# Splitting two of the seven products of a second layer once more, with their sums on GpSimd

## The chip, the cores and the metric

The kernel runs on one core of a Trainium2 chip. The metric is the device time of one execution in microseconds (us): the kernel before has a median of 1076.28 us over three executions (1075.8 to 1077.22).

Five engines work side by side, each through its own list of instructions in order: TensorE (PE; its weight loads are shown as PEld), VectorE (DVE), ScalarE (ACT), GpSimd (POOL) and SyncE (SP), which here only issues transfers. An engine waits for another through a semaphore. TensorE writes its results into PSUM banks; VectorE and ScalarE read them there. Transfers (DMA) are issued by SP or ACT and carried out by 16 DMA engines.

## The reference

An attention without softmax, normalised per head, followed by a gated feed-forward block:

```python
kv  = einsum('bhsd,bhse->bhde', k, v)            # batch 8, heads 8, seq 576, head_dim 64
out = einsum('bhsd,bhde->bhse', q, kv)
x   = out / rms(out) * g_norm                    # -> 4608 tokens x 512
gate = sigmoid(x @ w_gate)                       # 512 -> 1536
val  = x @ w_val
y    = (gate * val) @ w_out                      # 1536 -> 512, float32
```

The tokens are worked on in nine chunks of 512 (`c` = 0 to 8). Chunk 0 uses plain products. Chunks 1 to 8 have a "first layer" (`x @ w_gate`, `x @ w_val` and the gate) and a "second layer" (`@ w_out`), and in both the products are made by the scheme of Strassen and Winograd: a 2 x 2 block product with seven block products instead of eight, and with sums of blocks made beforehand (of the operands) and afterwards (of the results). In the second layer of a chunk the left operand is 512 tokens x 1536, the right one 1536 x 512; a block is 256 tokens x 768, or 768 x 256.

## The kernel before

Sums of the operands: `h_sums` (VectorE) makes `s12` and `s4` from the gated values `gv`; `t2w[1]` to `t2w[4]` are sums of blocks of `w_out`, made once. The second layer takes the tokens in two halves of a block (`g` = 0, 1; 128 tokens each) and makes seven products of six matmuls each (128 x 128 weights, 256 columns) per half:

```python
def second_layer_fast(c):
    b = {(j, n): w2[:, NF2 * (j - 1):NF2 * j, DH * (n - 1):DH * n] for j in (1, 2) for n in (1, 2)}
    for g in range(2):
        t1, t2 = slice(P * g, P * g + P), slice(GH + P * g, GH + P * g + P)
        (i_a, pa), (i_b, pb) = (take() for _ in range(2))        # PSUM banks
        last = (c, g) == (NG - 1, 1)
        parts = [slice(0, DH // 2), slice(DH // 2, DH)] if last else [slice(0, DH)]

        def product(ps, hs, ws, new):
            for f in range(NF2):                                 # 6 matmuls            (L870)
                nc.tensor.matmul(ps, hs(f), ws[:, f, :], start=(new and f == 0), stop=(f == NF2 - 1), ...)
                if f % 3 == 2:
                    slot()                                       # one step of other work

        product(pa, lambda f: gv[c, f][:, t1], b[1, 1], True)
        o2 = sg_tile()
        nc.scalar.copy(out=o2[:, d1], in_=pa)
        product(pb, lambda f: s12[c, f][:, t2], t2w[2], True)
        o1 = sg_tile()
        tt(out=o1[:, d2], in0=pb, in1=o2[:, d1], op=ALU.add)     # tt is VectorE
        product(pa, lambda f: gv[c, f + NF2][:, t1], b[2, 1], False)    # split by the change
        nc.scalar.copy(out=o1[:, d1], in_=pa)
        ...
        product(pb, lambda f: gv[c, f][:, t2], t2w[3], False)
        ...
        product(pc, lambda f: s12[c, f][:, t1], t2w[1][:, :, x], True)
        ...
        product(pb, lambda f: gv[c, f + NF2][:, t2], t2w[4], False)     # split by the change
        tt(out=o2[:, d1], in0=pb, in1=o2[:, d1], op=ALU.add)
        store(c, 2 + g, o2)
        ...
        product(pc, lambda f: s4[c, f][:, t1], b[2, 2][:, :, x], False)
        tt(out=o1[:, y], in0=pc, in1=o1[:, y], op=ALU.add)
        if last:
            store(c, g, o1, y, (nc.sync, nc.scalar))
        ...
        if not last:
            store(c, g, o1)
        if g == 1:
            load_late(c + 2)                                     # 12 loads of k and v, on SP
```

Result tiles come from the same four buffers as the tiles of the first layer, used in turn. A result tile is free again when the transfer that stores it has landed. The store cuts a tile of 128 tokens where the order of tokens jumps:

```python
def sg_tile():
    return sb.tile([P, G], FP32, tag="sg", name="sg", bufs=4)

def store(c, t, ot, cols=slice(0, DM), queues=(nc.sync,)):
    ...
        if b < 2:                                                # the first two batches  (L492)
            queues[i % len(queues)].dma_start(out=rows.rearrange("(p j) d -> j p d", j=NJ)[j, p:p + n],
                                              in_=ot[r0:r0 + n, cols])
        else:                                                    # all later ones         (L498)
            queues[i % len(queues)].dma_start(
                out=rows.rearrange("(r p g i) d -> i r g p d", p=QB, g=JH, i=2)[half, r, c0 // QB:(c0 + n) // QB],
                in_=ot[r0:r0 + n, cols])                         # QB = 32: shapes 32 x 512, 2x32x512, 3x32x512
```

The first layer of the next chunk begins like this (twelve `sg_tile`s in all, two for each of six steps `f`):

```python
def p1(d):
    d["ia"], d["pa"] = take()
    product(d["pa"], d["bg"][:, 0:NK], a[1, 1], True)            # 2 matmuls            (L728)
    d["u"] = d["sg"] = sg_tile()
    nc.scalar.copy(out=d["sg"][:, h2], in_=d["pa"])              #                       (L739)
...
    p1(one)
    p1(two)
    small(pd[:, q1], ones[:, NK], ax[:, 0, q1], True)            #                       (L732)
    nc.scalar.copy(out=g1[:, q1], in_=pd[:, q1])                 #                       (L791)
    small(one["pa"][:, q1], ones[:, NK + 1], ax[:, 1, q1], False)
    p6(one)
    small(pd[:, q1], tw2[2], s2[:, 1], False)
```

Beside the products run the attention of a later batch and the operand sums of the next chunk. Their steps are taken one at a time at each `slot()`. Those of weight: `x_turn` (L420, transposes on VectorE) followed by transfers `xT<-xTs` on SP (L430), and then `x_sums` (L691 to L704, VectorE), which need these transfers. GpSimd makes the weight sums of the first layer (`w_sum`, L720; `w_sums2`, L713).

Of the kernel before, what the change touches and what calls it, by code (L numbers as in the profile page):

```python
# [15 lines left out]
ALU = mybir.AluOpType  # L16
# [4 lines left out]
def kernel(  # L21
# [11 lines left out]
    nc = tc.nc  # L33

    B, H, S, HD = q.shape
    T, DM = out.shape
    DF = moe_w_gate.shape[1]
    P = 128
# [22 lines left out]
    NFT = DF // P  # L61
    G = 512
    GH = G // 2
    NG = T // G
# [40 lines left out]
    def load_late(b):  # L105


        if b >= B:
            return
        mains = {}  # L110
        for n in range(NHP):
            for name, src in (("k", k), ("v", v)):
                mains[n, name] = t = hp.tile([P, G], FP32, tag="gv", name="kv")
                nc.sync.dma_start(out=t.rearrange("p (h c) -> p h c", h=2),
                                  in_=src[b, 2 * n:2 * n + 2, 0:S4].rearrange("h (p j) d -> p h (j d)", j=NK4))
        rest = hp.tile([P, G], FP32, tag="gv", name="kv")
        for i, src in enumerate((k, v)):
            for r in range(2):
                nc.sync.dma_start(out=rest[PH * r:PH * r + PH, GH * i:GH * i + GH].rearrange("p (h d) -> p h d", d=HD),
                                  in_=src[b, NHP * r:NHP * r + NHP, S4:S].rearrange("h p d -> p h d"))  # L120
        kv_late[b] = mains, rest
# [213 lines left out]
    def slot():  # L335
        if fill:
            fill.popleft()()
# [122 lines left out]
    def spread(steps, at):  # L460

        n = 0
        for engine, step in steps:
            while engine == DVE and n < 7 * NF2 and n % 7 not in at:
                fill.append(idle)
                n += 1
            fill.append(step)
            n += 1

    def flush():  # L470
        while fill:
            fill.popleft()()

    gv = {}
# [5 lines left out]
# [5 lines that stand above are left out]
        r0 = i = 0  # L485
        while r0 < P:
            b, s = divmod(G * c + P * t + r0, S)
            rows = out[S * b:S * b + S, cols]
            if b < 2:
                j, p = divmod(s, NP)  # L490
                n = min(P - r0, NP - p)
                queues[i % len(queues)].dma_start(out=rows.rearrange("(p j) d -> j p d", j=NJ)[j, p:p + n],  # L492
                                                  in_=ot[r0:r0 + n, cols])
            else:
                half, c0 = divmod(s, S // 2)
                r, c0 = divmod(c0, XC)
                n = min(P - r0, XC - c0)
# [3 lines that stand above are left out]
            r0 += n  # L501
            i += 1
# [7 lines left out]
    def bank(i):  # L510
        return (psum_mm if i < 2 else psum).tile([P, 512], FP32, tag=f"mm{i}", name="mm")
# [3 lines left out]
    def mm0_ps():  # L515
        return bank(next(turns0) % 2)

    def mm_ps():
        return bank((2, 3, 0, 1)[next(turns) % 4])

    def at_ps():
        return psum.tile([P, NQ, 512], FP32, tag="at", name="at")
# [4 lines left out]
    def take():  # L527
        i = free.popleft()
        return i, bank(i)[:, 0:GH]

    def give(i):
        free.append(i)

    def early(n):

        shared = []

        def ps(kind):
            if kind == "q":
                return shared[0]  # L540
            t = psum0.tile([P, 2, 512], FP32, tag="kq" if kind == "kv" else f"ux{n % 2}", name="two")
            if kind == "kv":
                shared.append(t)
                return t[:, :, JH * P:]
            return t
        return ps
# [33 lines left out]
    a = [attention(n, early(n)) for n in range(NE)]  # L580
# [19 lines left out]
    for token in order.split():  # L600
        name = token.rstrip("0123456789.")
        n = [int(i) for i in token[len(name):].split(".")]
        f = n[0]
        if name == "b":
            if f not in blks:
                if f == 3:
                    psum_ctx.__exit__(None, None, None)
                    psum = ctx.enter_context(tc.tile_pool(name="psum", bufs=1, space=bass.MemoryType.PSUM))
                    ps = (mm_ps(), mm_ps())
                else:  # L610
                    ps = (mm0_ps() if f else warm, mm0_ps())
# [29 lines left out]
    for f in range(4, NFT):  # L641
        if f == NFT - 1:
            last = at_ps()
# [6 lines left out]
    ps = [mm_ps() for _ in range(G // P)]  # L650
# [22 lines left out]
    NF2 = NFT // 2  # L673
    DH = DM // 2
    h1, h2 = slice(0, GH), slice(GH, G)
    tt = nc.vector.tensor_tensor
    sx, tw, s12, s4 = {}, {}, {}, {}
# [171 lines left out]
    def h_sums(c, f):  # L849
# [5 lines left out]
        tt(out=one[:, h2], in0=one[:, h1], in1=one[:, h2], op=ALU.subtract)  # L855
        tt(out=s4[c, f], in0=two[:, h1], in1=s[:, h2], op=ALU.subtract)

    def second_layer_fast(c):
        b = {(j, n): w2[:, NF2 * (j - 1):NF2 * j, DH * (n - 1):DH * n] for j in (1, 2) for n in (1, 2)}
        d1, d2 = slice(0, DH), slice(DH, DM)  # L860
        for g in range(2):
            t1, t2 = slice(P * g, P * g + P), slice(GH + P * g, GH + P * g + P)
            (i_a, pa), (i_b, pb) = (take() for _ in range(2))

            last = (c, g) == (NG - 1, 1)
            parts = [slice(0, DH // 2), slice(DH // 2, DH)] if last else [slice(0, DH)]

            def product(ps, hs, ws, new):
                for f in range(NF2):
                    nc.tensor.matmul(ps, hs(f), ws[:, f, :], start=(new and f == 0), stop=(f == NF2 - 1),  # L870
                                     skip_group_check=True)
                    if f % 3 == 2:
                        slot()

            product(pa, lambda f: gv[c, f][:, t1], b[1, 1], True)
            o2 = sg_tile()
            nc.scalar.copy(out=o2[:, d1], in_=pa)
            product(pb, lambda f: s12[c, f][:, t2], t2w[2], True)
            o1 = sg_tile()
            tt(out=o1[:, d2], in0=pb, in1=o2[:, d1], op=ALU.add)  # L880
            product(pa, lambda f: gv[c, f + NF2][:, t1], b[2, 1], False)
            nc.scalar.copy(out=o1[:, d1], in_=pa)
            if last:
                store(c, g, o1, d1)
            product(pb, lambda f: gv[c, f][:, t2], t2w[3], False)
            tt(out=o2[:, d2], in0=pb, in1=o2[:, d1], op=ALU.add)
            pcs = []
            for x in parts:
                i_c, pc = take()
                pc = pc[:, 0:x.stop - x.start]  # L890
                pcs.append((i_c, pc))
                product(pc, lambda f: s12[c, f][:, t1], t2w[1][:, :, x], True)
                o2x = o2[:, DH + x.start:DH + x.stop]
                tt(out=o2x, in0=pc, in1=o2x, op=ALU.add)
            product(pb, lambda f: gv[c, f + NF2][:, t2], t2w[4], False)
            tt(out=o2[:, d1], in0=pb, in1=o2[:, d1], op=ALU.add)
            store(c, 2 + g, o2)
            give(i_a)
            give(i_b)
            for (i_c, pc), x in zip(pcs, parts):  # L900
                give(i_c)
                product(pc, lambda f: s4[c, f][:, t1], b[2, 2][:, :, x], False)
                y = slice(DH + x.start, DH + x.stop)
                tt(out=o1[:, y], in0=pc, in1=o1[:, y], op=ALU.add)
                if last:
                    store(c, g, o1, y, (nc.sync, nc.scalar))
            if not last:
                store(c, g, o1)
            if g == 1:
                load_late(c + 2)  # L910

    def sums_of(c):
        if c < NG:
            fill.append(lambda: fill.extendleft(reversed(x_sums(c))))
# [17 lines left out]
    t2w = {i: sums.tile([P, NF2, DH], FP32, name=f"t2w{i}", bufs=1) for i in (2, 3, 4)}  # L932
# [14 lines left out]
    for c in range(1, NG):  # L947
        if c + 1 < B:
            steps = feed(c + 1)
            if c == 1:  # L950

                i = 4
                while w2_sums:
                    steps.insert(i, (DVE, w2_sums.popleft()))
                    i += 3
            spread(steps, (1, 2, 3, 4, 5) if c == 1 else (2, 3, 4, 5))
        first_layer_fast(c)
        sums_of(c + 1)
        second_layer_fast(c)
        flush()  # L960
# [30 lines left out]
```

## Time and profile before

| | |
|---|---|
| time, median of three | 1076.28 us |
| profiled span | 1073.9 us |
| TensorE busy | 1062.2 us (99%) |
| VectorE busy | 712.0 us (66%) |
| GpSimd busy | 442.1 us (41%) |
| ScalarE busy | 309.0 us (29%) |
| granted TensorE clock | 0.998 |
| DMA, mean over the span | 60 GB/s |

The profile's first part gives busy time, the share of the span and the number of instructions of each engine; the second cuts the span into 40 slices and gives tenths of busy time; the fourth follows the chain of work that ended last back to the start. A float32 matmul appears in the trace as two records, so a product of six matmuls is 12 records. "SPq" is the issue of a transfer by SP; landing is later.

### The profile page before, as it was taken

To read this page: it belongs to the slowest core of one execution; us is meant where nothing else is said; L and a number is where in the kernel's file an instruction comes from. 1 tells how busy PE (TensorE), PEld (TensorE's weight loads), DVE (VectorE), ACT (ScalarE), POOL (GpSimd) and SP (SyncE) were. 2 spreads that over 40 slices of the span, in tenths; PEclk is the share of its full clock that TensorE was granted. 3 is DMA by queue.
4 is the path that set the end of the run, shared out by engine and by line. 5 is a ranking of instruction groups with operands and counts; after the bars stand their busy time and mean duration, and the time that the engine had idled before them with its cause. 6 is when DMAs were issued, how large, how long until landed. Compare 5 with 4: busy or idle time off the path is not lost.

```text
span 1073.9 us, 19464 instructions
## 1 busy us (share of the span) xinstructions
PE 1062.2 (99%) x7514; PEld 882.4 (82%) x7514; DVE 712.0 (66%) x1461; ACT 309.0 (29%) x737; POOL 442.1 (41%) x630
## 2 busy tenths in 40 slices
PE   8999999999999999999999999999999999999997
PEld 7544448888888888888888888888888888888886
DVE  4897767894579547863778357945786388628841
ACT  4654323331243113320433134312431122112210
POOL 0000035880367216640666046713663077307800
PEclk9999999999999999999999999999999999999999
DMA  9944710002400141012301140014001200010001
GB/s 259 254 157 157 244 29 22 24 17 60 119 12 13 45 128 36 12 35 62 100 23 34 42 120 13 25 45 137 13 12 27 58 2 1 2 38 1 1 1 40
DMA packets 69115, 64.96 MB, mean 60 GB/s; under 512 B 23712, under 2 KB 63008, under 8 KB 69024
## 3 DMA queue, kind: packets, MB, share of 16 engines
q1 hardware_dynamic: 68768, 63.69, 21.1%
q8 instruction: 60, 0.98, 0.4%
q14 instruction: 31, 0.25, 0.1%
q10 hardware_dynamic: 256, 0.03, 0.1%
HBM read 47.19 MB, written 9.44 MB: 53 GB/s over the span
## 4 chain that ended last, share of the span: by engine, by line
PE 97%; DVE 1%; DMA 1%; SPq 0%; issue 0%; ACT 0%; DVEq 0%
PE mm L728 46%; PE mm L870 27%; PE mm L732 7%; PE mm L556 7%; PE mm L653 4%; PE at L395 2%; PE at L354 1%; PE at L556 1%; DMA q<-in_q_dram 1%; PE two L291 0%; PE two L261 0%; PE mm L634 0%; PE two L318 0%; PE two L272 0%; PE at L360 0%; SPq L97 0%
## 5 line engine op out<-in xcount | busy, mean ns | idle before, releaser
L720 POOL TENSOR_TENSOR tw<-gv 128x256 f32<-128x256 f32 x192 | 156.2, 823 | 232.1 <-DVE w L202 145.0
L728 PE MATMUL mm<-xT,tw 128*128 128x256 f32 x768 | 198.4, 381 | 0.0
L728 PE MATMUL mm<-sx,tw 128*128 128x256 f32 x768 | 197.4, 380 | 0.0
L802 POOL TENSOR_TENSOR sg<-sg 128x256 f32<-128x256 f32 x48 | 35.6, 742 | 341.1 <-ACT sg L801 340.9
L720 POOL TENSOR_TENSOR tw<-gv,tw 128x256 f32<-128x256 f32 x192 | 155.0, 828 | 0.0
L728 PEld LDWEIGHTS mm<-xT,tw 128*128 128x128 f32 x768 | 137.3, 190 | 17.5 <-issue 2.9
L728 PEld LDWEIGHTS mm<-sx,tw 128*128 128x128 f32 x768 | 134.9, 191 | 12.4
L773 DVE TENSOR_TENSOR gv<-gv,sg 128x256 f32<-128x256 f32 x192 | 108.7, 585 | 0.0
L728 PE MATMUL mm<-sx,gv 128*128 128x256 f32 x384 | 91.2, 380 | 0.0
L728 PE MATMUL mm<-xT,gv 128*128 128x256 f32 x384 | 90.8, 379 | 0.0
L870 PE MATMUL mm<-w,gv 128*128 128x256 f32 x384 | 89.1, 381 | 0.7 <-DVE gv L773 0.7
L870 PE MATMUL mm<-t2w,gv 128*128 128x256 f32 x384 | 88.7, 381 | 0.0
L870 PE MATMUL mm<-w,s 128*128 128x256 f32 (+1 forms) x408 | 88.3, 367 | 0.0
L764 ACT ACTIVATE sg<-sg 128x256 f32<-128x256 f32 x96 | 40.0, 416 | 151.0 <-DVE sg L763 150.9
L739 ACT COPY sg<-mm 128x256 f32<-128x256 f32 x96 | 35.8, 373 | 162.7 <-PE mm L728 160.9
L870 PEld LDWEIGHTS mm<-w,gv 128*128 128x128 f32 x384 | 72.5, 190 | 12.2 <-DVE gv L773 2.5
L870 PEld LDWEIGHTS mm<-w,s 128*128 128x128 f32 x408 | 74.1, 190 | 9.4
L728 PEld LDWEIGHTS mm<-xT,gv 128*128 128x128 f32 x384 | 72.9, 190 | 10.4 <-issue 0.5
L728 PEld LDWEIGHTS mm<-sx,gv 128*128 128x128 f32 x384 | 72.5, 190 | 10.0
L870 PEld LDWEIGHTS mm<-t2w,gv 128*128 128x128 f32 x384 | 72.4, 190 | 10.0
L556 PE MATMUL mm<-xT,gv 128*128 128x512 f32 x176 | 77.4, 594 | 0.0
L745 DVE TENSOR_TENSOR gv<-mm,sg 128x256 f32<-128x256 f32 x96 | 37.0, 413 | 41.2 <-PE mm L728 37.8
(120 smaller groups left out, 1548.4 us busy)
## 6 DMA issues: line engine op xcount, KB each, us to landing
q<-in_q_dram SPq DMA_DIRECT2D x24, 288.0 KB
st<-in_moe_w_gate_dram SPq DMA_DIRECT2D x12, 512.0 KB
st<-in_moe_w_val_dram SPq DMA_DIRECT2D x12, 512.0 KB
st<-in_moe_w_out_dram SPq DMA_DIRECT2D x12, 512.0 KB
kv<-in_k_dram SPq DMA_DIRECT2D x24, 256.0 KB
kv<-in_v_dram SPq DMA_DIRECT2D x24, 256.0 KB
out_dram<-sg SPq DMA_DIRECT2D x23, 192.0 KB
xT<-xTs SPq DMA_DIRECT2D x48, 72.0 KB
```

Of the source, the lines that this page charges most:

```text
L395: nc.tensor.matmul(u[HD * e:HD * e + HD, r, o:o + HD], qTs[QB * r:QB * r + QB, (n0 + which) % 2, c:c + PH], kvq[QB * r:QB * r + QB, (n0 + ...
L556: nc.tensor.matmul(self.ps[i], w[("wg", "wv")[i], self.f][:, m, :], xT[self.c][:, m, :], start=(m == 0), stop=(m == NMT - 1), skip_group_c ...
L653: nc.tensor.matmul(ps[t], gv[0, f][:, P * t:P * t + P], w["wo", f], start=(f == 0), stop=(f == NFT - 1), skip_group_check=True)
L720: nc.gpsimd.tensor_tensor(out=tw[f, i], in0=b[in0], in1=b[in1] if isinstance(in1, tuple) else tw[f, in1], op=ALU.subtract)
L728: nc.tensor.matmul(ps, wt[:, m, :], xs[:, m, :], start=(new and m == 0), stop=(m == NK - 1), skip_group_check=True)
L732: nc.tensor.matmul(ps, wt, xs, start=new, stop=True, skip_group_check=True)
L739: nc.scalar.copy(out=d["sg"][:, h2], in_=d["pa"])
L745: tt(out=d["h"][:, h1], in0=d["pb"], in1=d["sg"][:, h2], op=ALU.add)
L764: nc.scalar.activation(out=d["sg"][:, h2], in_=d["sg"][:, h2], func=AF.Sigmoid)
L773: tt(out=d["h"][:, h], in0=d["h"][:, h], in1=d["sg"][:, h], op=ALU.mult)
L802: nc.gpsimd.tensor_tensor(out=g2[:, h1], in0=g2[:, h1], in1=g2[:, h2], op=ALU.add)
L870: nc.tensor.matmul(ps, hs(f), ws[:, f, :], start=(new and f == 0), stop=(f == NF2 - 1), skip_group_check=True)
```

## The change

It splits two of the seven block products of each second layer, the two that multiply the second halves of the gated values (`gv[c, f + NF2]`) by `b[2, 1]` and by `t2w[4]`, once more by the same scheme: each becomes seven products of three matmuls with 128 columns, over both halves of the tokens. That needs sums of quarter blocks: one set for each left operand (`sa4`, `sa2`) and one for each right operand (`tw4`, `tw2_`), each of four sums in three pieces of 128 x 128. GpSimd makes three sets, VectorE one. They are written over operands that have been used up. The right operand's sums are made anew for every chunk.

So the loop over `g` goes: both halves of a product are made before the next product, the two split products come last, and all four result tiles stay open until then. The two tiles `o2` are stored between the two splits, one on SP and one on ACT, and the two tiles `o1` at the end. One place in the first chunk spreads the making of `t2w` less widely (`i += 2`).

```diff
+    def sums2(engine, x, out, weights):
+        o = dict(zip((1, 2, 4, 3), out))
+        if weights:
+            ops = ((1, (1, 2), (1, 1)), (2, (2, 2), 1), (4, (2, 1), 2), (3, (2, 2), (1, 2)))
+        else:
+            o[3] = x[2, 1]
+            ops = ((1, (2, 1), (2, 2)), (2, 1, (1, 1)), (3, (1, 1), (2, 1)), (4, (1, 2), 2))
+        for i, in0, in1 in ops:
+            for j in range(N3):
+                ...
+                engine.tensor_tensor(out=o[i][j], in0=u0, in1=u1, ...)
 ...
+        for g in pair:
+            i_, pa = take()
+            product(pa, of(gv, lo, g), b[1, 1], True)
+            o2[g] = sg_tile()
+            nc.scalar.copy(out=o2[g][:, d1], in_=pa)
+            give(i_)
+        tw4 = sums2(nc.gpsimd, b4, thirds(of(gv, lo, 0) + of(gv, lo, 1)), True)
+        for g in pair:
+            i_b[g], pb[g] = take()
+            product(pb[g], of(s12, lo, 2 + g), t2w[2], True)
+            o1[g] = sg_tile()
+            nc.scalar.copy(out=o1[g][:, d1], in_=o2[g][:, d1])
+            tt(out=o1[g][:, d2], in0=pb[g], in1=o2[g][:, d1], op=ALU.add)
+        sa4 = sums2(nc.vector, a4, thirds(of(s12, lo, 2) + of(s12, lo, 3))[:3], False)
+        for g in pair:
+            product(pb[g], of(gv, lo, 2 + g), t2w[3], False)
 ...
+        sa2 = sums2(nc.gpsimd, a2, thirds(of(gv, lo, 2) + of(gv, lo, 3))[:3], False)
+        for g in pair:
+            i_c[g], pc[g] = take()
+            product(pc[g], of(s12, lo, g), t2w[1], True)
 ...
+        tw2_ = sums2(nc.gpsimd, b2, thirds(of(s12, lo, 0) + of(s12, lo, 1)), True)
+        for g in pair:
+            product(pc[g], of(s4, lo, g), b[2, 2], False)
+            tt(out=o1[g][:, d2], in0=pc[g], in1=o1[g][:, d2], op=ALU.add)
+            give(i_c[g])
+
+        def split(o, x, a, sa, w_, tw_, done=None):
+            (i_d, pd), (i_e, pe), (i_f, pf), (i_h, ph) = (take() for _ in range(4))
+            ...                                       # small(): 3 matmuls of 128 columns; add(): VectorE
+            small(pd, a[1, 1], w_[1, 1], True)
+            add(o[0][:, l], pd)
+            small(pf, a[1, 2], w_[2, 1], True)
+            add(o[0][:, l], pf)
+            slot()
+            small(pd, sa[2], tw_[2], False)
+            add(o[0][:, r], pd)
+            small(pe, sa[1], tw_[1], True)
+            add(o[1][:, r], pe)
+            slot()
+            small(pd, sa[3], tw_[3], False)
+            tt(out=y, in0=y, in1=pd.unsqueeze(1).to_broadcast([P, 2, P]), op=ALU.add)
+            small(ph, a[2, 2], tw_[4], True)
+            add(o[1][:, l], ph)
+            slot()
+            if done:
+                done()
+            small(pe, sa[4], w_[2, 2], False)
+            add(o[0][:, r], pe)
+            slot()
 ...
+        split(o2, d1, a4, sa4, b4, tw4)
+        for g, queue in zip(pair, (nc.sync, nc.scalar)):
+            store(c, 2 + g, o2[g], queues=(queue,))
+        if ends:
+            for g in pair:
+                store(c, g, o1[g], d2)
+            split(o1, d1, a2, sa2, b2, tw2_, lambda: [store(c, 1, o1[1], d1), store(c, 0, o1[0], tok[0])])
+            store(c, 0, o1[0], tok[1], (nc.sync, nc.scalar))
+        else:
+            split(o1, d1, a2, sa2, b2, tw2_)
+            for g in pair:
+                store(c, g, o1[g])
+        load_late(c + 2)
 ...
-                    i += 3
+                    i += 2
```

More of the change, by code (lines that the diff above doesn't have):

```diff
@@ L856, in h_sums @@
         tt(out=s4[c, f], in0=two[:, h1], in1=s[:, h2], op=ALU.subtract)
+    N3 = NF2 // 2
+    d1, d2 = slice(0, DH), slice(DH, DM)
+    tok = [slice(P * i, P * i + P) for i in range(G // P)]
+    def sums2(engine, x, out, weights):
[7 more added lines that the diff above has]
+            for j in range(N3):
+                u0, u1 = (x[n][j] if isinstance(n, tuple) else o[n][j] for n in (in0, in1))
+                engine.tensor_tensor(out=o[i][j], in0=u0, in1=u1,
+                                     op=ALU.add if i == 1 and not weights else ALU.subtract)
+        return o
@@ L858, in second_layer_fast @@
     def second_layer_fast(c):
         b = {(j, n): w2[:, NF2 * (j - 1):NF2 * j, DH * (n - 1):DH * n] for j in (1, 2) for n in (1, 2)}
[L860 to L870, printed above, removed]
-                                     skip_group_check=True)
[L872 to L910, printed above, removed]
@@ new lines, in second_layer_fast, with product, of, thirds @@
+        ends = c == NG - 1
+        pair = range(2)
+        lo, hi = range(NF2), range(NF2, NFT)
+        def product(ps, hs, ws, new):
+            for f in range(NF2):
+                nc.tensor.matmul(ps, hs[f], ws[:, f, :], start=(new and f == 0), stop=(f == NF2 - 1),
+                                 skip_group_check=True)
+                if f % N3 == N3 - 1:
+                    slot()
+        def of(tiles, fs, t):
+            return [tiles[c, f][:, tok[t]] for f in fs]
+        def thirds(tiles):
+            return [tiles[i:i + N3] for i in range(0, len(tiles), N3)]
@@ new lines, in h_quarters, with w_quarters @@
+        def h_quarters(tiles, fs, t):
+            return {(i, k): of(tiles, fs[N3 * (k - 1):N3 * k], t + i - 1) for i in (1, 2) for k in (1, 2)}
+        def w_quarters(ws):
+            return {(k, n): [ws[:, f, tok[n - 1]] for f in range(N3 * (k - 1), N3 * k)] for k in (1, 2) for n in (1, 2)}
+        a4, a2 = h_quarters(gv, hi, 2), h_quarters(gv, hi, 0)
+        b4, b2 = w_quarters(t2w[4]), w_quarters(b[2, 1])
+        o2, o1, pb, pc, i_b, i_c = {}, {}, {}, {}, {}, {}
+        for g in pair:
[4 more added lines that the diff above has]
+            give(i_)
@@ new lines, in second_layer_fast @@
+        tw4 = sums2(nc.gpsimd, b4, thirds(of(gv, lo, 0) + of(gv, lo, 1)), True)
[8 more added lines that the diff above has]
+            product(pb[g], of(gv, lo, 2 + g), t2w[3], False)
+            tt(out=o2[g][:, d1], in0=pb[g], in1=o2[g][:, d1], op=ALU.add)
+            give(i_b[g])
@@ new lines, in second_layer_fast @@
+        sa2 = sums2(nc.gpsimd, a2, thirds(of(gv, lo, 2) + of(gv, lo, 3))[:3], False)
+        for g in pair:
+            i_c[g], pc[g] = take()
+            product(pc[g], of(s12, lo, g), t2w[1], True)
+            tt(out=o2[g][:, d2], in0=pc[g], in1=o2[g][:, d1], op=ALU.add)
+        tw2_ = sums2(nc.gpsimd, b2, thirds(of(s12, lo, 0) + of(s12, lo, 1)), True)
[3 more added lines that the diff above has]
+            give(i_c[g])
@@ new lines, in split, with small, add @@
+        def split(o, x, a, sa, w_, tw_, done=None):
+            (i_d, pd), (i_e, pe), (i_f, pf), (i_h, ph) = (take() for _ in range(4))
+            pd, pe, pf, ph = (ps[:, 0:P] for ps in (pd, pe, pf, ph))
+            l, r = slice(x.start, x.start + P), slice(x.start + P, x.stop)
+            def small(ps, hs, ws, new):
+                for j in range(N3):
+                    nc.tensor.matmul(ps, hs[j], ws[j], start=(new and j == 0), stop=(j == N3 - 1),
+                                     skip_group_check=True)
+            def add(t, ps):
+                tt(out=t, in0=ps, in1=t, op=ALU.add)
+            small(pd, a[1, 1], w_[1, 1], True)
[9 more added lines that the diff above has]
+            small(pd, sa[3], tw_[3], False)
+            y = o[1][:, x].rearrange("p (n c) -> p n c", n=2)
+            tt(out=y, in0=y, in1=pd.unsqueeze(1).to_broadcast([P, 2, P]), op=ALU.add)
[6 more added lines that the diff above has]
+            add(o[0][:, r], pe)
+            slot()
+            for i in (i_d, i_f, i_h, i_e):
+                give(i)
```

## The prediction

> **What bounds the kernel now.** I read the busy times and the chain that ended last first.
>
> ```profile
> PE 1062.2 (99%) x7514; PEld 882.4 (82%) x7514; DVE 712.0 (66%) x1461; ACT 309.0 (29%) x737; POOL 442.1 (41%) x630
> PE 97%; DVE 1%; DMA 1%; SPq 0%; issue 0%; ACT 0%; DVEq 0%
> POOL 0000035880367216640666046713663077307800
> ```
>
> TensorE is busy for 99% of the span and the chain runs through it for 97%. So a matmul removed is worth its full time, and any wait added in front of TensorE costs its full time: there is no slack. The POOL row has zeros where the second layers lie: GpSimd is free there.
>
> The price of matmuls comes from TensorE's timeline in the last second layer, where wide products (256 columns, 12 records) stand beside one cut into two of 128 columns (24 records):
>
> ```profile
> 1055.20 2.75 PE L870 MATMUL mm<-t2w,gv 128*128 128x256 f32 x12
> 1057.79 2.84 PE L870 MATMUL mm<-w,s 128*128 128x128 f32 x24
> 1060.47 2.75 PE L870 MATMUL mm<-t2w,gv 128*128 128x256 f32 x12
> ```
>
> The first column is the start. 1057.79 - 1055.20 = 2.59 us for 12 wide records, 0.216 each; 1060.47 - 1057.79 = 2.68 us for 24 narrow ones, 0.1117 each. So weight loads keep up with narrow matmuls in a row (the 190 ns of a PEld is latency, not a limit), and a narrow matmul costs 0.517 of a wide one.
>
> **Next, the transfers**, because the change moves the stores. SP's timeline and the DMA view in chunk 7, where nothing else is transferred (that view cuts 942 to 952 into 40 slices of 0.25 us):
>
> ```profile
> 937.69 3.74 SPq L498 DMA_DIRECT2D out_dram<-sg  x4
> ...
> DMA  1201111101011111111111111111000000000000
> GB/s 74 57 25 49 49 41 33 25 16 33 33 49 57 49 49 57 49 49 49 49 49 57 49 57 49 49 49 41 25 25 0 0 0 0 0 0 0 0 0 0
> ```
>
> Two tiles of 256 KB are issued from 937.69 to 941.43, and data flow until slice 30, 949.5: 11.8 us after the first issue, at 49 GB/s with about 0.1 of 16 engines busy. The pair of chunk 8, issued from 1045.49, ends at 1056.4 in the same view: 10.9 us. One tile alone takes less; in chunk 4:
>
> ```profile
> 600.36 1.30 SPq L498 DMA_DIRECT2D out_dram<-sg  x2
> ...
> 606.43 3.78 SPq L430 DMA_DIRECT2D xT<-xTs  x6
> ```
>
> The issue at 606.43 is, in the built program, the one that waits for the first store (each transfer waits for the eighth before it), and the waits name that store for 0.6 us: one tile of shapes 3x32 and 32 lands 6.1 us after its issue. In chunk 5 (two pieces 2x32) the same reading gives 715.14 to 723.05, 7.9 us. All this is hidden before: a stored tile is reused twelve or more us later, so ScalarE's copy L739 at the start of the next layer waits for TensorE alone:
>
> ```profile
> 958.82 0.37 ACT L739 COPY sg<-mm 128x256 f32<-128x256 f32 x1 [10.81 <-PE mm L728]
> ```
>
> [...] 49 GB/s[...], against 305 to 385 GB/s in the k and v loads after chunk 2. [...] here 128x128 takes 482 to 635 ns on GpSimd (L713) and 280 on VectorE alone (L702)[...].
>
> **The change part by part.**
>
> *Removed and added matmuls.* Per chunk two products of 24 wide records go (2 x 24 x 0.216 = 10.37 us) and two of 42 narrow ones come (2 x 42 x 0.1117 = 9.38): 0.99 us. Eight chunks: 7.9. The cut products of the last chunk become whole: 48 x 0.1117 - 24 x 0.216 = 0.18. Gain: 8.1 us.
>
> *Sums on GpSimd.* 36 of about 0.55 us, 20 us per chunk in a second layer of 37 us where it is idle. Counting from the start of a second layer: tw4 can start at 5.4 (when both first products have read what it overwrites) and is done by 12, needed at 27.7; sa2 starts at 17.5, tw2_ follows at about 24 and ends at 30 to 31, its first half by 27.5; the second split wants them from 33.7. Off the path.
>
> *Sums on VectorE.* 12 x 0.2 us (L702 to L703 start 0.20 apart) = 2.4 us, ahead of the attention's transposes L420. Those start some 0.6 us later, but the store that stood before the xT transfers (1.3 us of issue) has gone, so xT is issued when it was. x_sums now stand in VectorE's list directly ahead of the additions of the first split, and in chunk 2 waited 3.9 us for xT before. With xT no longer behind stores I reckon 1 us of stalls in all.
>
> *The split's own waits.* pd is reused after two narrow products (1.34 us); the addition that frees it ends 0.67 + 0.2 + 0.28 = 1.15 us after its start. It fits, if barely.
>
> *Result tiles.* This is the step that decides. In the built program the first two copies L739 of the next layer wait for the stores of the two o2 tiles, since the four sg buffers are all in use. o2[1] is complete some 4.8 us before the end of the second layer, o2[0] 4.1, and both stores are issued then. [...] By the pairs above it has landed 11.5 us after the first issue where a 2x32 is in it (chunks 2, 4, 5, 7) and[...] about 9.2 where not (chunks 3, 6): 6.7 and 4.4 us after the end of the second layer. TensorE needs the first copy at 1.95 and, through the copy L791 that stands behind both in ScalarE's list, the second at 3.0, so landing has to be by about 1.5 and 2.3. Stalls: chunks 2 and 5 about 4.5 us, 3 and 6 about 2.2, 4 and 7 (where the slow type is the first to be waited for) about 5.5: 24 us. Chunk 1 stores through L492[...]: no stall.
>
> *Loads of k and v* wait behind eight transfers, four of them now late stores, up to 10 us beyond the end of the layer; the products that need them come at 16.3 plus the stall. Nearly hidden: 1.5 us.
>
> *The tail.* Before, 384 KB are issued from 1063.71 on and the data end 6.3 us after the last matmul. Now about 1 MB is issued from 4.8 us before the last matmul[...], so it ends 12 us after the last matmul. Cost: 5.5 us.
>
> Sum: 1076.3 - 8.1 + 1 + 24 + 1.5 + 5.5 = 1100. I predict 1096, a little below, because of the first rival.
>
> **The rivals.** First: the stores are no wait. If two queues do bring two tiles home in 6 us, stalls shrink to 1 us or none, the tail to 2 us: 1066 to 1074, faster. For it: the change names two queues, so somebody saw the store as tight. Against it: the pairs of chunks 7 and 8. Second: VectorE is the wait. If sa4 runs at 0.35 us per sum or xT lands as late as in chunk 2 before, x_sums hold the additions of the split, up to 3 us in six chunks: 10 to 15 us on top. Against it: VectorE has gaps of 4 to 5 us in each second layer. Third: GpSimd ends tw2_ late (over 0.7 us per sum), and the second split waits. That costs 2 us per chunk, but the lead of 6 us speaks against it.
>
> **Range and chances.** One chance in four that the stalls are small gives the low end; a full count of stalls, tail and some of the second rival the high end. 1072 to 1112. The 2% line upwards is 1097.8, next to my sum. Faster by over 2% would need 1054.8, more than the removed matmuls hold.
>
> **What would show it.** In the profile after: narrow records at 0.112 us and two splits of 4.7 us per chunk; the first L739 of chunks 3 to 8 waiting for a DMA of out_dram, not for TensorE, and TensorE (L732) idle behind ScalarE for 2 to 6 us there; none after chunk 1; POOL busy in second layers without anyone waiting for it; a span that ends about 12 us after the last matmul. I am wrong if L739 waits under 1 us (the first rival), or if TensorE's idle time stands before narrow matmuls behind VectorE (the second).

## The result and the profile after

The changed kernel takes 1123.0 us (median of four runs, 1121.2 to 1125.7) against 1076.5: a ratio of 1.043 (95% interval 1.041 to 1.046). The prediction was 1096 in a range of 1072 to 1112. It had the direction of its sum right and was 27 us short.

I set the two traces side by side layer by layer: on TensorE's timeline a first layer begins with a matmul of L728, a second layer with one of L870 (before) or L888 (after), and the tail is what follows the last matmul.

| us of the profiled span | before | after | difference | prediction's sum |
|---|---|---|---|---|
| start to the second layer of chunk 1 | 237.0 | 237.6 | +0.6 | 0 |
| eight second layers | 303.7 | 310.2 | +6.5 | -7.1 (matmuls -8.1, xT +1) |
| seven first layers between them | 525.2 | 556.7 | +31.5 | +25.5 (stores +24, loads +1.5) |
| tail | 8.0 | 14.5 | +6.5 | +5.5 |
| span | 1073.9 | 1119.0 | +45.1 | +23.9 |

The page of the changed kernel, in the parts shown of the one before:

```profile
PE 1071.8 (96%) x7778; PEld 893.8 (80%) x7778; DVE 782.1 (70%) x1651; ACT 307.8 (28%) x737; POOL 569.3 (51%) x918
...
POOL 0000037773577436681767156743668187908750
...
PE 83%; DMA 6%; DVE 6%; issue 1%; SPq 1%; ACT 1%; DVEq 0%; ACTq 0%; POOL 0%; POOLq 0%
```

GpSimd has filled the zeros, as meant. But the chain has left TensorE for 17% of the span, to transfers and VectorE. And TensorE is busy for 9.6 us more, although the change takes work from it: a first hint that it ran slower somewhere.

What TensorE itself waited for (us in all, times, longest):

```profile
PE mm L732 <- ACT sg L739: 11.0, 5, 4.6
PE mm L732 <- ACT sg L791: 9.9, 4, 3.8
PE mm L947 <- DVE sg L951: 7.9, 6, 2.0
PE mm L888 <- DVE sg L932: 1.8, 6, 0.3
```

The first two lie at the start of first layers, 20.9 us; the others in second layers, 9.7 us. Neither is the cause: ScalarE and VectorE pass on waits of their own. ScalarE's timeline after chunk 2, where the first layer begins at 396.10:

```profile
391.18 1.71 ACTq L498 DMA_DIRECT2D out_dram<-sg  x2
398.64 0.37 ACT L739 COPY sg<-mm 128x256 f32<-128x256 f32 x1 [23.43 <-DMA out_dram<-sg]
403.37 0.37 ACT L739 COPY sg<-mm 128x256 f32<-128x256 f32 x1 [4.35 <-DMA out_dram<-sg]
```

The o2 tile that ACT issues at 391.18 (32 and 3x32 rows) lands at about 398.6. The other, two pieces of 2x32 issued by SP at 391.98, lands at 403.3, 11.3 us later. TensorE stands for 0.85 and 3.54 us behind these copies. The chain shows the same hold as one step of 10.59 us.

### The profile page after: what moved, and what is told of

Read it like the earlier page. It is cut to its first block, busy times and chain, and to the rows that moved or that the text cites. A ratio compares the mean times of both kernels' runs of the same rounds, so it can differ in the third digit from the quotient of the medians.

```text
span 1119.0 us, 20676 instructions
## 1 busy us (share of the span) xinstructions
PE 1071.8 (96%) x7778; PEld 893.8 (80%) x7778; DVE 782.1 (70%) x1651; ACT 307.8 (28%) x737; POOL 569.3 (51%) x918
## 4 chain that ended last, share of the span: by engine, by line
PE 83%; DMA 6%; DVE 6%; issue 1%; SPq 1%; ACT 1%; DVEq 0%; ACTq 0%; POOL 0%; POOLq 0%
PE mm L728 44%; PE mm L888 12%; PE mm L732 7%; PE mm L556 7%; DMA out_dram<-sg 5%; PE mm L653 4%; PE mm L947 4%; DVE s L876 2%; PE at L395 2%; PE at L354 1%; SPq L430 1%; DMA xT<-xTs 1%; PE mm L634 1%; DVE gv L876 1%; DVE xTs L420 1%
## 5 line engine op out<-in xcount | busy, mean ns | idle before, releaser
L728 PE MATMUL mm<-sx,tw 128*128 128x256 f32 x768 | 202.9, 388 | 0.0
L728 PE MATMUL mm<-xT,tw 128*128 128x256 f32 x768 | 198.6, 381 | 0.0
L728 PEld LDWEIGHTS mm<-xT,tw 128*128 128x128 f32 x768 | 137.4, 191 | 18.0 <-issue 3.4
L728 PEld LDWEIGHTS mm<-sx,tw 128*128 128x128 f32 x768 | 138.3, 195 | 13.2
L773 DVE TENSOR_TENSOR gv<-gv,sg 128x256 f32<-128x256 f32 x192 | 110.8, 596 | 0.0
L739 ACT COPY sg<-mm 128x256 f32<-128x256 f32 x96 | 35.8, 373 | 271.5 <-DMA out_dram<-sg 164.0
L728 PE MATMUL mm<-sx,gv 128*128 128x256 f32 x384 | 91.2, 380 | 0.0
L728 PE MATMUL mm<-xT,gv 128*128 128x256 f32 x384 | 90.8, 379 | 0.0
L888 PE MATMUL mm<-w,s 128*128 128x256 f32 x384 | 85.8, 381 | 1.8 <-DVE sg L932 1.8
L745 DVE TENSOR_TENSOR gv<-mm,sg 128x256 f32<-128x256 f32 x96 | 37.1, 413 | 71.3 <-PE mm L728 69.6
L888 PEld LDWEIGHTS mm<-w,s 128*128 128x128 f32 x384 | 72.5, 190 | 13.9 <-DVE sg L932 4.2
L728 PEld LDWEIGHTS mm<-sx,gv 128*128 128x128 f32 x384 | 72.5, 190 | 10.0
L728 PEld LDWEIGHTS mm<-xT,gv 128*128 128x128 f32 x384 | 72.3, 190 | 10.0 <-issue 0.5
L556 PEld LDWEIGHTS mm<-xT,gv 128*128 128x128 f32 x176 | 32.6, 190 | 37.4 <-issue 35.9
L763 DVE TENSOR_TENSOR sg<-mm,sg 128x256 f32<-128x256 f32 x96 | 40.7, 424 | 30.8 <-PE mm L728 30.5
L749 DVE TENSOR_TENSOR gv<-mm,gv 128x256 f32<-128x256 f32 x96 | 40.4, 420 | 29.4 <-PE mm L728 28.2
L713 POOL TENSOR_TENSOR tx<-gv,tx 128x128 f32<-128x128 f32 x96 | 53.3, 556 | 7.5
```

Source lines behind the costliest of these rows:

```text
L556: nc.tensor.matmul(self.ps[i], w[("wg", "wv")[i], self.f][:, m, :], xT[self.c][:, m, :], start=(m == 0), stop=(m == NMT - 1), skip_group_c ...
L713: nc.gpsimd.tensor_tensor(out=tw2[i], in0=in0, in1=tw2[in1] if isinstance(in1, int) else in1, op=ALU.subtract)
L728: nc.tensor.matmul(ps, wt[:, m, :], xs[:, m, :], start=(new and m == 0), stop=(m == NK - 1), skip_group_check=True)
L749: tt(out=d["h"][:, h2], in0=ps, in1=d.pop("u")[:, h2], op=ALU.add)
L763: tt(out=d["sg"][:, h2], in0=d["pb"], in1=d["sg"][:, h2], op=ALU.add)
L773: tt(out=d["h"][:, h], in0=d["h"][:, h], in1=d["sg"][:, h], op=ALU.mult)
```

## The experiments

All times are medians. The runs stood on three chips, each beside the kernel before on its own chip (1076.1 to 1076.4 us); "less" and "more" are against the changed kernel's 1123.0. Theory 1 is the prediction's own: late stores hold the four result buffers. Theory 2 is its second rival: VectorE is late.

**e1: the o2 tiles of chunks 2 to 7 are not stored.** It leaves out those rows of the output and nothing else.

```diff
-        for g, queue in zip(pair, (nc.sync, nc.scalar)):
+        for g, queue in zip(pair, (nc.sync, nc.scalar)) if c in (1, NG - 1) else ():
```

> The changed kernel, but in chunks 2 to 7 the two tiles of the second token half (o2) are not stored: those rows of the output are left out, all arithmetic stays. Theory 1 (late stores hold the four result buffers): the copies at the start of the next first layer no longer wait for a transfer, the first layers after chunks 2 to 7 come back from 74 to 84 us to 71.5 to 76.5, together 31 us, so about 1092 us. The second layers and the tail stay as they are. Theory 2 (VectorE and GpSimd slow each other and xT comes late, and that is the greater part): 1110 to 1123. A third, that the lower clock has its own cause: the waits go (-20 us) but PEclk still falls to 0.82 to 0.86 for 8 us or more at the start of the first layers, 1100 to 1105.

Measured: 1093.1 us, 30 less than the changed kernel. The first layers take 528.1 us together instead of 556.7; second layers (310.9) and tail (14.2) stay. Theory 1 holds for the first layers, and it is not the stores of o2 that lengthen the second ones. TensorE's granted clock rose with it, from 0.985 to 0.993 over the span, so most of that loss hangs on the waits. Here is that clock, in the changed kernel, over the first 30 us of the first layers after chunks 2 to 7. The columns are the window, its length, the busy time of five engines, then the granted clock (1.00 is full), the DMA share and GB/s:

```profile
396.10:426.10 30.00, 25.61 (x193) 22.23 (x192) 14.31 (x33) 8.18 (x23) 11.28 (x16) 0.94 0.39 118
518.50:548.50 30.00, 28.08 (x212) 24.52 (x211) 17.52 (x41) 10.47 (x30) 15.03 (x23) 1.00 0.40 117
636.40:666.40 30.00, 25.39 (x186) 22.16 (x185) 13.49 (x31) 8.12 (x23) 10.69 (x15) 0.89 0.39 118
760.50:790.50 30.00, 26.14 (x195) 22.57 (x194) 14.54 (x34) 8.18 (x23) 11.62 (x17) 0.94 0.40 118
881.80:911.80 30.00, 28.15 (x148) 24.77 (x147) 19.10 (x43) 8.80 (x25) 17.68 (x26) 1.00 0.09 28
991.20:1021.20 30.00, 25.64 (x127) 22.69 (x126) 15.37 (x36) 6.34 (x20) 13.94 (x21) 0.94 0.09 30
```

The shortfalls 0.06, 0.11, 0.06 and 0.06 of 30 us make 8.7 us lost to the clock; with the 20.9 us of waits that is 29.6 of the 31.5. The dips stand in just those four layers whose longest pause of TensorE was 3.5 to 4.6 us; where it was 1.3 us (chunks 3 and 6) there is none. After chunk 4, finer windows show the clock at half:

```profile
640.00:644.00 4.00, 0.91 (x3) 0.91 (x4) 0.00 (x0) 0.91 (x3) 0.00 (x0) 0.80 0.35 101
644.00:648.00 4.00, 4.00 (x13) 3.28 (x13) 0.42 (x1) 0.27 (x1) 0.00 (x0) 0.50 0.74 224
648.00:652.00 4.00, 4.00 (x19) 3.54 (x18) 2.98 (x8) 2.13 (x4) 1.45 (x2) 0.84 0.78 257
```

The pause ended at 643.10 and TensorE was busy without a break from then on, but at half speed until about 649: four wide records (L728) take 1.71 us from 643.68 on and 0.87 us from 649.67 on. The shortfalls 0.20, 0.50 and 0.16 of 4 us are 3.4 us lost, so 6.9 us at half; after chunk 2, where 1.8 us were lost, about half as long. In the second layer of chunk 1 a pause of 2.01 us was followed by half clock too (see the last section).

**e2: stores in pieces of 32 rows.**

```diff
-                n = min(P - r0, XC - c0)
+                n = min(P - r0, XC - c0, QB)
```

> The changed kernel with every store cut into pieces of 32 rows[...]. Theory 1: eight pieces of o2 on two queues are issued within 3 us and land about 2 us later, before TensorE needs the buffers; the waits of the first layers go (-31 us) and the tail shrinks by 4 to 6 us: about 1087 us. Rival (the time from issue to landing is latency, or issuing eight pieces takes as long as two slow transfers): stalls stay above half, 1105 to 1123. The second layers lose 0 to 2 us more, as the k and v loads stand behind more issues.

Measured: 1082.5 us, 40.5 less. All first layers are back at their time before (525.2 us), and the tail is 7.6. The stores of L498 are twice as many (120 instead of 60) with the same bytes; what differs is the busy share of the DMA engines. Here are the busy share of the 16 engines in tenths and the transfer rate in two stretches of 10 us, cut into 40 slices of 0.25 us, from 391 in the changed kernel and from 390 here; the o2 stores are issued from 391.2 on in both:

```profile
DMA  0000910013021012115212111143324967422222
GB/s 0 0 0 0 213 49 0 0 41 33 8 33 16 25 33 57 41 57 147 74 49 66 49 57 74 74 131 107 98 57 123 197 197 254 139 98 82 90 82 74
```

```profile
DMA  0000000091888969581000200000027399776666
GB/s 0 0 0 0 0 0 0 0 221 41 213 205 221 353 180 295 139 205 25 0 0 0 66 0 0 33 0 0 0 57 188 90 254 295 238 238 148 164 156 172
```

Above, after a first burst, a trickle, mostly at 8 to 74 GB/s and mostly with 0.1 or 0.2 of the 16 engines busy; the next stores run into it. Below, 0.5 MB at about 190 GB/s with mostly 0.8 or 0.9 of the engines busy, done by 394.75, before the layer ends at 396. So the 11 us were not the time that these bytes need, but that of a transfer with mostly 0.1 or 0.2 of the engines busy.

**e3: all four sets of sums on GpSimd.**

```diff
-        sa4 = sums2(nc.vector, a4, thirds(of(s12, lo, 2) + of(s12, lo, 3))[:3], False)
+        sa4 = sums2(nc.gpsimd, a4, thirds(of(s12, lo, 2) + of(s12, lo, 3))[:3], False)
```

> The changed kernel with all four sets of sums on GpSimd, the one of VectorE too. Theory 2 (the twelve sums on VectorE take 0.46 us apiece instead of 0.2 because GpSimd makes its own beside them, and put off the transposes, xT, the sums of x and so the additions of the first split): the second layers of chunks 1 to 6 fall from 38.8 to 41.9 us towards 37.5, together 8 to 13 us: about 1112 us; the waits for stores stay. If the late xT comes from elsewhere (transfers, ScalarE): 1119 to 1123. GpSimd then makes 48 sums, 21 us, and ends them at 31 us of a second layer; if it is late for the second split, each second layer gains up to 2 us: 1120 to 1130.

Measured: 1110.0 us, 13.1 less. Second layers fall to 37.6 us (chunks 1 to 6) and 35.5: together 296.7, 7.0 under the kernel before, which is the split's promised gain. The first layers keep their waits (559.4). So theory 2 is true as well, and for another part of the time: two causes, not one.

How the twelve sums did it is read from VectorE's timeline of the changed kernel in chunk 2:

```profile
368.84 1.21 DVE L876 TENSOR_TENSOR s<-gv 128x128 f32<-128x128 f32 x3
369.97 1.46 DVE L876 TENSOR_TENSOR s<-s,gv 128x128 f32<-128x128 f32 x3
371.36 1.46 DVE L876 TENSOR_TENSOR gv<-gv 128x128 f32<-128x128 f32 x3
372.74 1.46 DVE L876 TENSOR_TENSOR s<-gv,s 128x128 f32<-128x128 f32 x3
374.12 0.74 DVE L404 TENSOR_REDUCE ms<-sqs 128x9 f32<-128x576 f32 x1
...
386.49 0.69 DVE L691 TENSOR_TENSOR sx<-xT 128x512 f32<-128x512 f32 x1 [4.05 <-DMA xT<-xTs]
```

and GpSimd's of the same stretch:

```profile
368.97 5.54 POOL L876 TENSOR_TENSOR gv<-gv 128x128 f32<-128x128 f32 x12 [3.31 <-PE mm L888]
```

From 368.84 to 374.12 VectorE makes twelve sums, 0.44 us each. GpSimd's set sa2 runs beside them all the way. The attention's work (L404, then the transposes L420) stands behind: counted from the start of the second layer, the transposes end after 22.9 us instead of 19.7 in e3. VectorE stands idle for 4.05 us until xT has come, and x_sums (L691) start after 30.6 us instead of 27.5. The additions of the split stand behind x_sums, and TensorE waits for those (1.95 us before its matmuls at 387.86). In chunks 7 and 8 the twelve sums are just as slow (5.5 and 5.4 us; 5.4 in chunk 2), but there is no attention left to stand behind them, and both second layers take 35.4 and 35.6 us as in e3: it is the chain that turns slow sums into lost time.

**Is it GpSimd's company? Its set sa2 left out.** The second split then takes quarters that aren't summed, so part of the computation is left out; all matmuls, additions and stores remain.

```diff
-        sa2 = sums2(nc.gpsimd, a2, ...)
+        sa2 = {1: a2[1, 1], 2: a2[2, 1], 3: a2[1, 2], 4: a2[2, 2]}
```

> The changed kernel without the set of sums sa2 on GpSimd (12 of its 36 sums): the second split takes unsummed quarters of the same size, so its values leave a part of the computation out, and all matmuls, additions and stores stay. VectorE then makes its own set sa4 with GpSimd idle or at work on the weights' sums only. If VectorE's sums took 0.46 us because GpSimd worked beside them, they now take about 0.2 us (at most those that meet the next set tw2_ stay slow), the transposes come 3 us sooner and the second layers of chunks 1 to 6 fall to about 37.6 us: 1110 us. If 0.46 us is the price of such a sum on VectorE whoever works beside it, it stays 0.46 and the time 1121 to 1123.

Measured: 1107.9 us; second layers 37.6 and 35.5 us, as in e3, though VectorE makes its own set here. Its timeline, the same twelve sums:

```profile
364.78 0.69 DVE L876 TENSOR_TENSOR s<-gv 128x128 f32<-128x128 f32 x3
365.38 0.69 DVE L876 TENSOR_TENSOR s<-s,gv 128x128 f32<-128x128 f32 x3
365.99 0.69 DVE L876 TENSOR_TENSOR gv<-gv 128x128 f32<-128x128 f32 x3
366.59 0.68 DVE L876 TENSOR_TENSOR s<-gv,s 128x128 f32<-128x128 f32 x3
367.20 0.74 DVE L404 TENSOR_REDUCE ms<-sqs 128x9 f32<-128x576 f32 x1
```

2.42 us from the first to L404: 0.20 us each, the prediction's figure. So the sums are not slow and the engine isn't overloaded; it is GpSimd's company that doubles them: 0.20 us becomes 0.44, while GpSimd's go from 0.42 (5.00 us for twelve in e3) to 0.46. One sum of each takes 0.44 to 0.46 us side by side, less than 0.20 + 0.42, and nearly all of the delay falls on VectorE. VectorE's additions L745, with one input in PSUM, took 406 to 425 ns in the changed kernel and 406 to 426 before; the four of 96 that lie wholly beside a GpSimd operation took 409 ns in the median.

The trace of the kernel before had this price already, in a line that I did not read for it:

```profile
L773 DVE TENSOR_TENSOR gv<-gv,sg x192: 378/546/950, 173.8 to 1030.4; 128x256 f32<-128x256 f32 x192
```

These are shortest, median and longest time in ns of a VectorE operation with two inputs in SBUF. The nine that meet no GpSimd operation take 410 to 419 ns; the 111 that lie wholly beside one take 614 in the median and up to 950.

**The order without the split.** Both halves side by side, four tiles open, o2 stored late by two queues, but the two products whole, without any of the new sums (one line of several; both splits go, and the four calls of `sums2`):

```diff
-        split(o2, d1, a4, sa4, b4, tw4)
+        whole(o2, d1, 2, t2w[4])        # for g in (1, 0): 6 matmuls of 256 columns, then one addition
```

> The order of the changed kernel (both pairs of tokens side by side, four tiles open, the first two stored late by two queues), but the two products are not split: 24 wide matmuls each, no narrow ones and none of the sums. Theory 1 and 2 together: the split itself gains 8 us, so these come back (+8); no sums on VectorE and GpSimd in the second layer (-10 to -13); the waits for stores stay within 0.5 us per chunk: about 1118 us. If it is the narrow matmuls or their many additions that cost the time, it falls to 1075 to 1090.

Measured: 1089.3 us, and a miss of my expectation by 29: I had the waits stay, and they fell to a third. First layers take 536.1 us instead of 556.7, second layers 302.8, the tail 11.3. The trace says why. A whole product finishes one half's tile and then the other's, so its stores are issued 2.6 us apart, at 383.39 (ACT) and 385.98 (SP) against a layer's end at 390.50. A split works on both tiles until its last product, and its stores are issued 0.8 us apart and only 4.9 and 4.1 us before the end. That this difference is the reason is read from the two traces; no run moved the stores alone. What remains in chunk 2 is one pause:

```profile
395.62 0.46 PE L732 MATMUL mm<-sx,tx 128*128 128x128 f32 x2 [1.92 <-ACT sg L791]
```

1.92 us, after which the granted clock stays at 1.00. So the new order costs 13 us by itself, and the split makes of those waits ones of up to 4.6 us, and behind the four of 3.5 us and more the clock was at half.

**One queue for both o2 tiles.**

```diff
-        for g, queue in zip(pair, (nc.sync, nc.scalar)):
+        for g, queue in zip(pair, (nc.sync, nc.sync)):
```

> The changed kernel with both o2 tiles stored from SP alone, no second queue. Theory 1: [...]the second queue is worth only that the second tile is issued 1.3 us sooner: 1120 to 1127. If the two queues get in each other's way[...] (or ScalarE's issues hold up its copies): 1105 to 1118. If the second queue is worth a good deal: over 1130.

Measured: 1129.1 us, 6 more than with two queues, a little outside what I gave theory 1. SP issues o2[0] first and the tile that was ready before it, o2[1], behind it: four issues in 2.84 us from 392.75, where two queues were done in 2.1 (391.18 to 393.26). After chunk 2 the first copy L739 comes 9.3 us after the first issue (7.5 with two queues), the second 12.1 (12.2). So the second queue brings the earlier tile's issue forward; the pair as a whole lands no sooner for it. Most of the difference is the clock again: in the traces the waits of the first layers grow from 20.9 to 24.4 us, and half clock covers 30.7 us of these layers instead of 17.1, which is another 6.8 us lost.

**Five result buffers instead of four.**

```diff
-        return sb.tile([P, G], FP32, tag="sg", name="sg", bufs=4)
+        return sb.tile([P, G], FP32, tag="sg", name="sg", bufs=5)
```

> The changed kernel with five result buffers instead of four, stores and sums unchanged[...]. The first copy of the next first layer now takes the free buffer, the second waits for the tile that ScalarE's queue stored first, the third for SP's some 15 us later. Theory 1: that tile lands some 7 us after its issue where it has no 2x32 piece (chunks 2, 3, 5, 6: stalls under 1 us) and some 11 us where it has (chunks 4, 7: still 4 us); so about 22 of the 31 us go, with the halved clock in chunks 2 and 5: 1098 to 1102 us. If the number of buffers isn't it: over 1115.

Measured: 1106.1 us, 17 less and not 22. The waits after chunks 4 and 7 remain, as reckoned, and after chunk 7 half clock still follows the pause (3.42 us; that layer takes 78.0 us instead of 71.5); after chunk 4 it does not follow one of 3.57 us. The buffer's reuse is the wait; one buffer more mends half of it.

**Both mends together**, e2 and e3.

> The changed kernel with both mends: stores in pieces of 32 rows and all four sets of sums on GpSimd. If the two causes are separate, their gains add up: 1123 - 40.5 - 13.1 = 1069.5 us, that is, first layers of 76.4 and 71.5 us as before the change, second layers of 37.6 and 35.5, and a tail of 7.6: 7 us under the kernel before, which is what the removed matmuls hold. If they are one cause seen twice (the late xT also put off what a store needed, or the other way round): 1076 to 1082.

Measured: 1069.0 us (ratio to the kernel before 0.993, interval 0.992 to 0.994), as the sum had it. TensorE is back at 99% busy, and no wait of it behind ScalarE or VectorE in the layers is left. The copies that waited for stores wait for TensorE again:

```profile
390.34 0.37 ACT L739 COPY sg<-mm 128x256 f32<-128x256 f32 x1 [24.61 <-PE mm L728]
391.21 0.37 ACT L739 COPY sg<-mm 128x256 f32<-128x256 f32 x1 [0.49 <-PE mm L728]
```

**The control: the kernel before with pieces of 32 rows.**

> A control: the kernel before with stores in pieces of 32 rows, nothing else. Theory: before, no store was waited for, so only the tail and the xT behind the stores can gain: 1072 to 1076. If the pieces alone bring 5 us or more, part of the gain of the mended kernel has nothing to do with the split.

Measured: 1072.2 us (0.996, interval 0.995 to 0.998). Layers as before; only the tail shrinks, from 8.0 to 4.0 us. So the pieces bring the mended kernel nothing in the layers: its 7.1 us there are the split's. Against this control, though, it is only 3.2 us faster, since its tail of 7.6 us is 3.6 longer.

**The mended kernel, its last pieces issued by two engines in turn.**

```diff
-                store(c, g, o1[g], d2)
+                store(c, g, o1[g], d2, (nc.sync, nc.scalar))
```

and likewise for the two stores in the last split.

> The mended kernel (pieces of 32 rows, all sums on GpSimd) with the last chunk's o1 pieces issued by SP and ScalarE in turn, since SP alone issues 22 of them from 1055.8 to 1065.9 us while the last matmul is over at 1060.2. If issuing sets the end, the tail falls from 7.6 us to about 4.5, as in the kernel before with pieces (4.05): 1066 us. If the data do (0.5 MB still under way), it stays 1068 to 1069.

Measured: 1066.0 us (0.990, interval 0.989 to 0.992), the tail 4.6. SP now issues 14 pieces from 1055.33 to 1062.33 instead of 22 until 1065.9. This is the fastest version: 1% under the kernel before, 0.6% under the control.

## Why the prediction was wrong, step by step

*Matmuls, -8.1.* Right in kind, a little too large. With the sums off VectorE the second layers are 7.0 us shorter, and 0.7 of that is a wait that is gone (in the kernel before TensorE stood for L773 from 239.28 to 239.99, in chunk 1). In the kernel with both mends, 84 narrow records take 9.56 us in the last chunk, 0.1138 each instead of 0.1117: 0.18 us per chunk, 1.4 in all, which is most of the 1.8 that are missing.

*Sums on VectorE, "1 us of stalls in all": the step that failed most.* It reads "12 x 0.2 us" and "Those start some 0.6 us later"; the sums took 0.44 us, and the transposes ended 3.2 us later. The second layers lost 6.5 + 7.0 = 13.5 us there (1.7 of it at half clock in chunk 1, whose mean is 0.96 over 41.85 us). The 0.2 us came from sums that ran alone, and the same text had sa2 start "at 17.5", well after them. But GpSimd starts when the first tiles that it overwrites have been read, 13.1 us into the second layer of chunk 2, at the same moment as sa4 (13.0 us in). The price is twice 0.2 in such company. The second rival named the consequence with its size ("10 to 15 us on top") and I put it aside because VectorE had gaps of 4 to 5 us; gaps were no help, since what was late stood in a chain from L404 over the transposes and xT to L691. The sign that it had named for this rival is in the profile: TensorE idle before narrow matmuls (L947) behind VectorE, 7.9 us.

*The stores' hold, +24.* Right in mechanism, in the order of the chunks and nearly in size: the waits of TensorE are 20.9 us, longest after chunks 4 (4.6 us) and 7 (4.4), shortest after 3 and 6. Its landing time of 9.2 us for chunks 3 and 6 was an estimate of mine that no run showed. No stall after chunk 1 was right: the 0.5 MB of its o2 tiles moved in 2.2 us (275.7 to 277.9), mostly with 0.8 or 0.9 of the DMA engines busy, and TensorE has no wait in the first 20 us of that first layer. What the sum lacked is the term that follows a long wait: 8.7 us at half the clock.

*Loads of k and v, +1.5.* No wait for them is among TensorE's in the changed kernel. *Tail, +5.5:* 6.5; it ends 14.5 us after the last matmul, not 12. My 12 us were an estimate, but what they reckoned with, slow transfers, is the larger part: pieces of 32 rows alone bring the tail to 7.6.

*The shading.* From 1100 down to 1096 "because of the first rival". That rival was wrong: the waits are for stores, and two queues did not make them fast.

So the 21 us between a predicted difference of 23.9 and the 45.1 of the spans are xT and VectorE 12.5, the clock 8.7 less what the waits and loads fell short (2.7), the tail 1.0, matmuls 1.1 and the start 0.6. Times outside the profile are some 2 to 4 us above the spans.

## What to carry to other kernels

When a change moves a store later, ask by when its buffer is wanted again and what share of the DMA engines is busy while it runs; cutting it into pieces of 32 rows, which raised that share from 0.1 or 0.2 to mostly 0.8 or 0.9, took 40 us off here. When it gives work to GpSimd, look at what VectorE does in the very same microseconds: a sum that took 0.20 us alone took 0.44 in company. And a wait of TensorE has to be counted with what follows it: here 20.9 us of waits brought another 8.7 us of lost clock. Which pause brought it was not told by its length alone, as the next section shows.

## What the runs showed of the hardware

In the layers of the changed kernel the granted clock was 0.50 or 1.00. It was 0.50 from 270.36, 403.48, 642.41, 768.71 and 997.40 us on, each time for 3.41 us, but for 6.83 us from 642.41. The distances between these starts are 39, 70, 37 and 67 times 3.413 us, so I laid steps of that length over this trace's matmuls. TensorE stood idle for 2.01 to 3.41 us in the steps just ahead of these five dips, and for no more than 1.45 us in any other step of the layers. The least, 2.01 us, is one pause inside one step (267.62 to 269.63). With five buffers a pause of 3.57 us (634.89 to 638.46) lies across two steps, 1.67 us before 636.56 and 1.90 us after it, and no dip followed. The columns are as in the clock table above, the first two lines from the changed kernel, the others from the one with five buffers:

```profile
266.95:270.36 3.41, 1.40 (x12) 1.24 (x12) 2.00 (x5) 0.00 (x0) 0.00 (x0) 1.00 0.12 29
270.36:273.77 3.41, 3.41 (x18) 3.41 (x17) 1.72 (x5) 0.00 (x0) 0.00 (x0) 0.50 0.02 5
...
633.15:636.56 3.41, 1.74 (x10) 1.24 (x9) 0.42 (x1) 0.00 (x0) 0.00 (x0) 1.00 0.24 73
636.56:639.97 3.41, 1.51 (x9) 1.41 (x10) 0.00 (x0) 0.81 (x3) 0.00 (x0) 1.00 0.45 135
639.97:643.38 3.41, 3.41 (x20) 3.05 (x19) 3.06 (x8) 2.13 (x4) 1.41 (x2) 1.00 0.74 207
```

The dip of two steps is the one in whose first step TensorE stood idle for 0.68 us; in the four of one step it was 0.48 us or less. So a dip cost 1.7 or 3.4 us, and a pause of 2.01 us had one behind it and a pause of 3.57 us none. This is read from the traces; no run was made to test it, and the cause was not shown.
